# Renumbered MLP units, a merged w_in transfer and a new order in a fused attention and MLP kernel

## The chip, the core and the metric

The kernel runs on one core of a Trainium2 chip. The metric is the device time of one execution in microseconds (us); lower is better.

## The reference

Attention with normalized q and k over 8 batches of 12 heads (448 positions, head width 64), and then an MLP with a hard-swish gate on the 3584 x 768 result. All inputs and the output are float32.

```python
q_n, k_n = rmsnorm(q, g_q), rmsnorm(k, g_k)          # over the last axis
scores = (1.0 / np.sqrt(64)) * np.matmul(q_n, k_n.transpose(0, 1, 3, 2))
attn = softmax(scores)
x = np.matmul(attn, v).transpose(0, 2, 1, 3).reshape(3584, 768)
h = x @ w_in                                          # w_in: 768 x 2048
g = h * np.clip(h + 3.0, 0.0, 6.0) / 6.0
out = g @ w_out                                       # w_out: 2048 x 768
```

## The kernel before

The work goes by pairs of heads: 6 pairs a batch, 48 in all. For a pair, SyncE loads q, k and v (tiles `qk` and `vf`), squares are taken (tile `sq`, line 364 on ACT, 366 on POOL), DVE sums them (`ssq`, lines 488 and 454), ACT makes the inverse roots with a logarithm and an exponential (`rs`, lines 430 and 433), and q and k are scaled to bf16 (`qks`, line 369, on POOL or DVE). They are transposed to `T`, for the early pairs by TensorE (line 542) and copies out of PSUM (lines 352 and 360), for later pairs by a DMA transpose from SyncE's queue (line 561). The scores (lines 617 and 594) go to the PSUM tiles `S` and `X`, ACT takes their exponential (`eT`, lines 622 and 600), and the product with the values (`va`, with a column of ones for the sum) goes to `XF` or `X` (lines 639 and 680). DVE divides (line 655 or 699), and the result, transposed, is `xT`, the MLP's input (lines 664 and 715 on TensorE, 706 by DMA).

The first batch is done in two halves of 224 query positions, so that the MLP can begin early. Its hidden units are made by `h_first` (line 753): eight calls c = 0 to 7 for each half, each for two blocks of 128 units, so 224 columns to a matmul. All other batches use `h_group` (line 772): one block of 128 units, 448 columns. ACT and DVE then make the gate (lines 731 and 734) and write `gT`, with the hidden units on the partitions. `y_group` (line 794) multiplies 128 rows of `gT` with `w_out`, 16 blocks of 128 units, in two halves of 384 output columns, and the sum is copied to `y` and stored (lines 350, 352 and 815).

Both weight matrices are loaded once by GpSimd's queue, which turns float32 into bf16 on the way: w_in in four transfers of 512 columns (line 825), w_out in four transfers of 512 rows (line 830). In w_out, hidden unit c * 512 + f * 128 + p lies on partition p, so a partition receives four separate rows of 768 from one transfer. The blocks of units of w_in are 128 neighbouring columns:

```python
f0 = (2 * c + f) * 128
em(nc.tensor.matmul(out=ps()[:, f * SH:(f + 1) * SH], lhsT=w_in_sb[:, kt, f0:f0 + 128], ...))
```

No instruction is emitted where its function stands. Every step is entered in a `Plan` with what it reads and writes and the engines that it may run on. At the end `plan.emit(ORDER)` emits the 2386 steps in the order of a list written out in the file, each on the engine that the table `WAY` gives (0, the first of its list, where it isn't named). `em` ties each instruction to the one before it on the same engine, so that each engine, and each DMA queue, runs its steps strictly in that order. A step that waits holds up all that is queued behind it on its engine.

Where TensorE has nothing to do at the start, 30 matmuls on zeros are entered (`warm`, line 382), and 32 more (`idle`, line 375) in the first batch's value products.

Of the kernel before, what the change touches and what calls it, by code (L numbers as in the profile page):

```python
# [9 lines left out]
BF16 = mybir.dt.bfloat16  # L10
# [13 lines left out]
    53: 1, 54: 1, 61: 1, 63: 2, 68: 1, 69: 1, 83: 1, 84: 1, 90: 2, 95: 1, 101: 1, 121: 1, 122: 1, 128: 2,  # L24
    148: 1, 155: 2, 212: 1, 230: 1, 248: 1, 358: 1, 386: 1, 387: 1, 393: 2, 462: 1, 469: 1, 481: 1, 486: 1,
    523: 1, 531: 2, 553: 1, 560: 2, 573: 1, 589: 2, 608: 1, 618: 1, 624: 2, 653: 2, 664: 1, 738: 1, 770: 1,
    776: 2, 795: 1, 821: 1, 822: 1, 860: 2, 886: 2, 921: 1, 949: 1, 982: 1, 1005: 1, 1010: 1, 1024: 1, 1049:
    1, 1056: 1, 1067: 1, 1082: 2, 1108: 1, 1140: 2, 1151: 1, 1166: 1, 1177: 1, 1269: 1, 1285: 1, 1286: 1,
    1292: 1, 1317: 1, 1324: 2, 1350: 2, 1361: 1, 1369: 1, 1370: 1, 1376: 1, 1408: 2, 1419: 1, 1434: 1, 1445:
    1, 1469: 1, 1497: 1, 1530: 1, 1553: 1, 1565: 1, 1572: 2, 1589: 1, 1597: 1, 1604: 2, 1624: 1, 1630: 2,  # L30
    1641: 1, 1649: 1, 1656: 2, 1673: 1, 1682: 1, 1688: 1, 1714: 1, 1725: 1, 1754: 1, 1785: 1, 1817: 1, 1822:
    1, 1872: 1, 1892: 1, 1898: 2, 1917: 1, 1918: 1, 1924: 2, 1949: 1, 1956: 1, 1964: 1, 1979: 2, 1987: 1,
    2011: 1, 2039: 1, 2067: 1, 2072: 1, 2095: 1, 2100: 1, 2107: 1, 2108: 1, 2114: 2, 2143: 1, 2159: 1, 2160:
    1, 2166: 1, 2195: 1, 2250: 1, 2281: 1, 2345: 1, 2350: 1, 2362: 1, 2374: 1,
# [3 lines left out]
    9, 20, 8, 21, 22, 11, 23, 10, 24, 25, 14, 26, 13, 27, 53, 17, 31, 55, 32, 16, 33, 28, 54, 91, 34, 56,  # L38
    58, 57, 35, 68, 92, 61, 36, 59, 12, 70, 60, 29, 69, 62, 212, 15, 73, 71, 214, 64, 72, 119, 74, 37, 83,
    30, 66, 213, 76, 38, 39, 118, 65, 84, 40, 75, 67, 41, 230, 85, 18, 102, 77, 104, 103, 93, 42, 94, 79,  # L40
    215, 81, 43, 146, 80, 86, 44, 95, 45, 82, 87, 145, 105, 96, 129, 88, 46, 19, 122, 231, 131, 121, 89,
    224, 47, 63, 48, 97, 49, 232, 120, 98, 106, 130, 110, 111, 99, 107, 108, 112, 233, 132, 113, 109, 114,
    100, 123, 156, 216, 50, 148, 51, 149, 133, 115, 157, 135, 52, 78, 134, 116, 158, 136, 124, 0, 90, 217,
    137, 234, 125, 172, 159, 117, 138, 150, 139, 126, 140, 173, 164, 174, 141, 165, 142, 127, 151, 160, 235,
    166, 152, 175, 161, 153, 162, 143, 167, 163, 144, 101, 188, 168, 190, 169, 154, 248, 176, 128, 180, 189,
    218, 178, 170, 181, 177, 182, 219, 191, 183, 179, 171, 200, 184, 236, 220, 185, 201, 202, 221, 250, 245,
    155, 192, 186, 193, 203, 340, 222, 225, 187, 303, 251, 204, 223, 226, 194, 304, 249, 195, 237, 305, 242,
    196, 205, 359, 252, 197, 306, 238, 206, 243, 239, 315, 198, 240, 316, 227, 339, 207, 199, 317, 208, 228,
    241, 307, 253, 209, 308, 318, 327, 254, 341, 246, 309, 310, 271, 255, 328, 272, 367, 210, 273, 360, 311,
    329, 211, 229, 342, 312, 347, 343, 330, 319, 147, 256, 320, 344, 313, 321, 322, 314, 348, 274, 257, 349,  # L50
    361, 345, 331, 332, 350, 258, 370, 333, 334, 323, 1, 371, 324, 372, 275, 335, 259, 325, 276, 336, 362,
    373, 374, 489, 326, 337, 263, 375, 338, 363, 397, 387, 364, 351, 376, 398, 378, 352, 377, 353, 354, 379,
    365, 355, 399, 386, 356, 401, 264, 400, 357, 402, 380, 2, 388, 500, 358, 381, 403, 501, 405, 346, 265,
    406, 404, 407, 408, 389, 490, 382, 277, 502, 409, 383, 506, 390, 503, 410, 384, 266, 391, 385, 411, 267,
    507, 268, 412, 278, 504, 508, 3, 505, 512, 283, 513, 392, 509, 491, 510, 535, 284, 511, 525, 514, 269,
    515, 516, 524, 517, 492, 270, 518, 493, 285, 519, 537, 520, 366, 286, 279, 538, 494, 521, 280, 536, 526,
    291, 495, 281, 522, 541, 292, 523, 282, 533, 543, 293, 539, 260, 287, 527, 540, 294, 368, 288, 544, 528,
    261, 542, 545, 529, 289, 546, 393, 547, 247, 548, 290, 564, 582, 497, 566, 549, 565, 299, 550, 244, 530,
    300, 567, 395, 551, 295, 532, 301, 552, 572, 553, 498, 302, 570, 554, 296, 573, 394, 571, 421, 297, 583,
    568, 593, 595, 569, 298, 422, 423, 4, 555, 424, 594, 413, 414, 415, 496, 425, 596, 416, 531, 417, 5,  # L60
    418, 574, 419, 426, 575, 556, 601, 427, 420, 599, 618, 576, 428, 429, 602, 584, 430, 557, 577, 559, 431,
    433, 578, 585, 600, 432, 434, 558, 579, 607, 586, 437, 435, 580, 617, 438, 581, 436, 597, 439, 6, 605,
    441, 598, 606, 588, 440, 442, 608, 628, 443, 603, 7, 630, 604, 445, 444, 587, 619, 446, 631, 609, 610,
    646, 447, 611, 636, 629, 612, 637, 449, 647, 613, 620, 614, 659, 450, 660, 737, 448, 615, 634, 738, 453,
    616, 635, 451, 750, 632, 452, 657, 633, 454, 739, 458, 658, 648, 638, 621, 459, 740, 623, 460, 649, 741,
    622, 650, 748, 639, 749, 640, 641, 743, 663, 455, 751, 642, 643, 461, 651, 456, 262, 462, 652, 590, 644,
    457, 470, 645, 562, 465, 742, 561, 664, 466, 369, 754, 591, 756, 560, 661, 471, 760, 662, 467, 770, 665,
    626, 666, 757, 667, 769, 668, 625, 472, 669, 795, 396, 670, 473, 655, 589, 796, 671, 474, 468, 654, 672,
    755, 771, 786, 752, 782, 753, 482, 761, 483, 772, 783, 777, 797, 758, 499, 780, 773, 759, 484, 775, 745,
    469, 485, 821, 774, 798, 762, 781, 486, 763, 764, 765, 854, 812, 822, 477, 766, 624, 799, 677, 800, 767,  # L70
    478, 534, 823, 853, 746, 808, 806, 784, 809, 778, 479, 787, 801, 592, 807, 855, 678, 844, 480, 785,
    1017, 832, 481, 824, 834, 825, 788, 679, 829, 789, 879, 673, 680, 835, 768, 790, 653, 791, 1018, 833,
    674, 813, 685, 563, 675, 792, 802, 793, 686, 627, 826, 676, 810, 803, 687, 840, 838, 856, 464, 811, 681,
    827, 688, 804, 1019, 682, 857, 859, 656, 814, 683, 815, 816, 845, 794, 839, 693, 880, 684, 817, 841,
    694, 818, 744, 747, 819, 689, 1020, 695, 858, 870, 866, 696, 836, 867, 690, 881, 1075, 701, 888, 691,
    702, 837, 896, 692, 864, 776, 892, 703, 842, 882, 697, 843, 704, 830, 698, 488, 883, 709, 885, 699, 887,
    846, 1021, 865, 700, 710, 820, 1023, 871, 847, 711, 848, 705, 1050, 893, 712, 861, 849, 706, 1049, 850,
    1076, 851, 717, 707, 852, 890, 884, 708, 1030, 868, 1051, 718, 869, 713, 1040, 719, 897, 872, 891, 873,
    874, 720, 875, 487, 714, 1052, 1031, 876, 877, 725, 715, 878, 1028, 894, 716, 726, 895, 1077, 721, 1029,
    722, 860, 1078, 898, 723, 899, 1036, 727, 1034, 724, 900, 1053, 1035, 901, 1054, 729, 902, 903, 1037,  # L80
    730, 1022, 728, 904, 1032, 731, 1060, 1062, 1055, 1061, 733, 732, 1041, 734, 1025, 1033, 1134, 905, 886,
    1083, 735, 1038, 1066, 828, 1079, 1086, 1063, 736, 906, 1080, 909, 1039, 463, 1081, 1088, 907, 910,
    1109, 908, 1042, 862, 1101, 911, 1043, 1044, 1026, 1087, 913, 912, 1133, 831, 1045, 1089, 914, 1046,
    475, 917, 1135, 1067, 1092, 918, 915, 1047, 919, 1102, 1057, 916, 1112, 1114, 1027, 1064, 1103, 920,
    1065, 805, 922, 1110, 921, 1160, 923, 1058, 1068, 1093, 1048, 1069, 1113, 924, 925, 779, 929, 926, 889,
    1070, 1104, 1105, 1124, 1118, 1115, 1106, 1071, 930, 1072, 1285, 1073, 933, 1107, 931, 1084, 934, 1119,
    932, 863, 1159, 1090, 1120, 935, 476, 1144, 937, 1136, 1091, 936, 1150, 938, 1161, 941, 939, 1074, 1094,
    1056, 940, 1095, 942, 1162, 1286, 945, 943, 1142, 1121, 1096, 944, 1097, 946, 1098, 1024, 1099, 950,
    1137, 1163, 1145, 1125, 1165, 947, 1287, 1146, 1138, 1170, 1116, 1147, 948, 1139, 1117, 951, 949, 952,
    1317, 1318, 1176, 1288, 1122, 1172, 1123, 1082, 957, 1319, 1100, 953, 1151, 958, 1289, 954, 1290, 1126,  # L90
    1320, 1141, 959, 1127, 961, 1294, 1171, 1164, 960, 1128, 1129, 1173, 962, 1130, 1344, 1308, 1131, 965,
# [870 lines left out]
```

## Time and profile before

| | |
|---|---|
| median of 3 runs | 423.66 us (423.53 to 423.99) |
| the profiled execution | 423.13 us, its span 421.4 us |
| instructions in the span | 9981 |
| TensorE matmul, busy | 413.0 us (98%) |
| ACT, busy | 288.3 us (68%) |
| DVE, busy | 233.1 us (55%) |
| POOL, busy | 168.8 us (40%) |
| granted TensorE clock | 0.999 |
| DMA, mean rate | 161 GB/s |

PE is TensorE's matmul side and PEld its weight loads, which run beside the matmuls. DVE is VectorE, ACT ScalarE, POOL GpSimd, SP SyncE. A q behind the name (POOLq, SPq) is an engine's queue that issues DMAs. "L753" is line 753 of the kernel. q0 is the DMA queue that GpSimd fills (the weights), q1 the one of SyncE and ACT. Busy times of a group are the time in which at least one of its instructions runs; matmuls overlap, so that a busy time divided by a count is the distance from one to the next, and the mean duration beside it is longer. Line numbers of the kernel after are larger by 1 to 9 from line 262 on.

### The profile page before, as it was taken

The page shows a single profiled execution, that of the slowest core. Times are in us where ns is not written, and L with a number is a line of the kernel's source. Part 1 is how long each engine was busy: PE and PEld are TensorE (multiplying, and loading weights), DVE is VectorE, ACT ScalarE, POOL GpSimd, SP SyncE. Part 2 cuts the span into 40 slices and gives each one's busy share as a digit, 9 for nine tenths or more (in the row PEclk, how much of TensorE's full clock was granted, in tenths as well). Part 3 has the DMA queues.
Part 4 walks back from the last instruction along what each step waited for, and adds up shares of the span by engine and source line. Part 5 has one row for each costly group of instructions (what it writes and reads, how often), then busy time and mean ns, then how long its engine had stood idle before and what let it go on. Part 6 is the DMA issues. An engine that isn't in the chain of part 4 may idle for free.

```text
span 421.4 us, 9981 instructions
## 1 busy us (share of the span) xinstructions
PE 413.0 (98%) x3959; PEld 243.8 (58%) x3960; DVE 233.1 (55%) x474; ACT 288.3 (68%) x527; POOL 168.8 (40%) x189
## 2 busy tenths in 40 slices
PE   7899999999999999999999999999999999999996
PEld 3566886555545555555555555555655556555565
DVE  5987776588875667536554754447345333333210
ACT  6999887678887988788767876677765662133201
POOL 3999596478374554427344143043210100000000
PEclk9999999999999999999999999999999999999999
DMA  7999999999779799568495683747350601120034
GB/s 241 319 282 196 258 216 177 275 268 271 178 194 252 193 252 242 111 154 211 115 224 160 164 206 73 135 154 166 82 93 12 143 2 47 30 81 27 8 107 114
DMA packets 98979, 67.77 MB, mean 161 GB/s; under 512 B 53204, under 2 KB 95476, under 8 KB 98932
## 3 DMA queue, kind: packets, MB, share of 16 engines
q1 hardware_dynamic: 93296, 60.50, 56.9%
q0 software_dynamic: 5248, 6.29, 9.0%
q8 instruction: 31, 0.51, 0.5%
q10 hardware_dynamic: 388, 0.34, 0.3%
q14 instruction: 16, 0.13, 0.1%
HBM read 50.23 MB, written 11.01 MB: 145 GB/s over the span
## 4 chain that ended last, share of the span: by engine, by line
PE 82%; DMA 7%; ACT 5%; DVE 2%; issue 1%; POOL 1%; SPq 1%; POOLq 0%; ACTq 0%; DVEq 0%
PE M L772 27%; PE M L794 25%; PE X L680 9%; PE S L594 5%; PE M L753 4%; DMA qk<-in_k_dram 4%; PE S L794 4%; PE X L594 3%; DMA T<-qks 2%; PE X L772 1%; ACT sq L364 1%; DMA out_dram<-y 1%; ACT eT L600 1%; ACT eT L622 1%; PE S L617 1%
## 5 line engine op out<-in xcount | busy, mean ns | idle before, releaser
L794 PE MATMUL M<-w_out_sb,gT 128*128 128x384 bf16 x752 | 139.3, 326 | 0.2 <-DMA w_out_sb<-in_moe_w_out_dram 0.2
L772 PE MATMUL M<-xT,w_in_sb 128*128 128x448 bf16 x618 | 135.0, 353 | 0.1
L369 POOL TENSOR_TENSOR qks<-qk,rs 112x512 bf16<-112x512 f32 (+1 forms) x91 | 91.0, 1019 | 107.3 <-ACT rs L433 77.2
L794 PEld LDWEIGHTS <-gT 128*128 128x128 bf16 x912 | 84.5, 98 | 59.5 <-issue 7.6
L734 DVE SCALAR_TENSOR_TENSOR gT<-ts,M 128x448 bf16<-128x448 f32 x119 | 73.2, 616 | 72.1 <-ACT ts L731 71.6
L600 ACT ACTIVATE eT<-S 112x896 bf16<-112x896 f32 x112 | 100.3, 915 | 15.7 <-PE S L594 8.5
L731 ACT ACTIVATE ts<-M 128x448 f32<-128x448 f32 x119 | 64.7, 545 | 42.7 <-PE M L772 29.2
L772 PEld LDWEIGHTS <-w_in_sb 128*128 128x128 bf16 x672 | 60.2, 98 | 56.3 <-issue 10.5
L366 POOL TENSOR_TENSOR sq<-qk 112x512 f32<-112x512 f32 (+1 forms) x57 | 58.0, 1024 | 52.9 <-DMA qk<-in_q_dram 29.7
L680 PEld LDWEIGHTS <-eT 112*128 112x128 bf16 x1344 | 52.7, 97 | 14.5 <-issue 2.0
L600 ACT ACTIVATE eT<-X 112x896 bf16<-112x896 f32 x56 | 51.3, 917 | 13.3 <-PE X L594 12.2
L680 PE MATMUL X<-va,eT 112*128 112x65 bf16 x1344 | 56.0, 194 | 0.1
L454 DVE TENSOR_REDUCE ssq<-sq 112x16 f32<-112x1024 f32 x42 | 50.9, 1213 | 6.1 <-POOL sq L366 4.7
L594 PE MATMUL S<-T 64*128 64x448 bf16 x224 | 34.0, 353 | 0.1
L352 DVE COPY y<-M 128x384 f32<-128x384 f32 x26 | 14.5, 556 | 30.9 <-PE M L794 30.8
L699 DVE TENSOR_TENSOR xn<-X,rd 112x512 bf16<-112x512 f32 x42 | 28.9, 689 | 1.3 <-DVE rd L696 0.2
L696 DVE RECIPROCAL rd<-X 112x8 f32<-112x8 f32 x42 | 8.6, 206 | 34.5 <-PE X L680 28.6
L594 PEld LDWEIGHTS <-T 64*128 64x128 bf16 x336 | 12.9, 94 | 24.5 <-issue 17.2
L364 ACT ACTIVATE sq<-qk 112x512 f32<-112x512 f32 (+1 forms) x40 | 23.0, 586 | 2.8 <-DMA qk<-in_k_dram 2.5
L350 ACT COPY y<-M 128x384 f32<-128x384 f32 x21 | 10.0, 477 | 19.4 <-PE M L794 19.2
L753 PE MATMUL M<-xT,w_in_sb 128*128 128x224 bf16 x192 | 22.9, 259 | 0.0
L794 PE MATMUL S<-w_out_sb,gT 128*128 128x384 bf16 (+1 forms) x128 | 22.6, 316 | 0.0
(87 smaller groups left out, 300.9 us busy)
## 6 DMA issues: line engine op xcount, KB each, us to landing
qk<-in_k_dram SPq DMA_DIRECT2D x45, 256.0 KB, 4.8
qk<-in_q_dram SPq DMA_DIRECT2D x45, 256.0 KB, 4.7
vf<-in_v_dram SPq DMA_DIRECT2D x43, 256.0 KB, 4.8
w_in_sb<-in_moe_w_in_dram POOLq DMA_DIRECT2D x4, 768.0 KB, 8.4
w_out_sb<-in_moe_w_out_dram POOLq DMA_DIRECT2D x4, 768.0 KB, 9.5
out_dram<-y SPq DMA_DIRECT2D x7, 336.0 KB, 3.5
out_dram<-y SPq DMA_DIRECT2D x8, 288.0 KB, 3.3
out_dram<-y SPq DMA_DIRECT2D x8, 240.0 KB, 2.8
```

What stands on the lines that cost most here:

```text
L366: em(nc.gpsimd.tensor_tensor(out=out, in0=in_, in1=in_, op=A_MULT))
L369: em((nc.vector if e == DVE else nc.gpsimd).tensor_tensor(out=out, in0=in_, in1=by.unsqueeze(3).to_broadcast(list(in_.shape)), op=A_MULT))
L454: em(nc.vector.tensor_reduce(out=ssq[:].rearrange("p i n -> p (i n)"), in_=sq[:].rearrange("p i (n d) -> p (i n) d", d=D), axis=AX_X, op=A ...
L594: em(nc.tensor.matmul(out=ps[:, a, 0:S], lhsT=qkT[r, S + t * TP:S + t * TP + 128], rhs=qkT[r, 0:S], start=True, stop=True))
L600: em(nc.scalar.activation(out=eT[:, t, 0:S2].rearrange("p (a s) -> p a s", a=2), in_=ps[0:TP, :, 0:S], func=EXP, bias=0.0, scale=1.0))
L680: em(nc.tensor.matmul(out=X_ps[:, a, i * E1:(i + 1) * E1], lhsT=eT[:, t, c:c + 128], rhs=va[:, a, t, :], start=(t == 0 and i == 0), stop=( ...
L699: em(nc.vector.tensor_tensor(out=xn[:].rearrange("p i a d -> p a i d"), in0=view()[:, :, :, 0:D], in1=rd[:].unsqueeze(3).to_broadcast([TP, ...
L731: em(nc.scalar.activation(out=ts[:], in_=ps()[:, 0:S], func=RELU, bias=0.5, scale=1.0 / 6.0))
L734: em(nc.vector.scalar_tensor_tensor(out=out, in0=shape(ts[:]), scalar=1.0, in1=shape(ps()[:, 0:S]), op0=A_MIN, op1=A_MULT))
L753: em(nc.tensor.matmul(out=ps()[:, f * SH:(f + 1) * SH], lhsT=w_in_sb[:, kt, f0:f0 + 128], rhs=xT[:, kt, z * SH:(z + 1) * SH], start=(kt == ...
L772: em(nc.tensor.matmul(out=ps()[:, 0:S], lhsT=w_in_sb[:, kt, f * 128:(f + 1) * 128], rhs=xT[:, kt, :], start=(kt == 0), stop=(kt == NKT - 1)))
L794: em(nc.tensor.matmul(out=ps()[:, 0:nc0], lhsT=gT[:, f, i * 128:(i + 1) * 128], rhs=w_out_sb[:, f, c0:c0 + nc0], start=(f == 0), stop=(f = ...
```

## The change

It has three parts.

1. The hidden units are numbered anew. In w_out, unit c * 512 + 4 p + f now lies on partition p, so that a partition's four rows of one transfer lie one after another in memory: 12 KB in one piece. To match, the block f of 128 units takes every fourth column of w_in, from column f mod 4 of chunk f div 4 on (new function `hid`). The weights of the 864 hidden matmuls are thus read with a step of four elements.
2. `w_in` is three tiles instead of one, and is loaded in three transfers instead of four: 512, 1024 and 512 columns (`WIN`).
3. `ORDER` and `WAY` are written anew. There is one step fewer, so all numbers from 2 on move by one. Apart from that, the last 383 steps stand as before, and so do the first 23; in between the order differs, most in the first half. 72 steps run on another engine: of note are the casts of v (GpSimd has 16 of them instead of 7), and a few squares, copies and scalings.

The lists of numbers in `ORDER` and `WAY` are left out here.

```diff
-    w_in_sb = const.tile([128, NKT, DFF], BF16, name="w_in_sb")
+    WIN = ((0,), (1, 2), (3,))
+    w_in_sb = [const.tile([128, NKT, len(cs) * 512], BF16, name=f"w_in_sb{cs[0]}") for cs in WIN]
...
+    def hid(f, kt):
+        c, r = divmod(f, 4)
+        i = next(i for i, cs in enumerate(WIN) if c in cs)
+        c -= WIN[i][0]
+        return w_in_sb[i][:, kt, c * 512 + r:(c + 1) * 512:4]
...
-                        f0 = (2 * c + f) * 128
                         em(nc.tensor.matmul(
-                            out=ps()[:, f * SH:(f + 1) * SH], lhsT=w_in_sb[:, kt, f0:f0 + 128],
+                            out=ps()[:, f * SH:(f + 1) * SH], lhsT=hid(2 * c + f, kt),
...
-                        out=ps()[:, 0:S], lhsT=w_in_sb[:, kt, f * 128:(f + 1) * 128],
+                        out=ps()[:, 0:S], lhsT=hid(f, kt),
...
-        for c in range(4):
-            def f_i(_, c=c):
-                cols = slice(c * 512, (c + 1) * 512)
+        for i, cs in enumerate(WIN):
+            def f_i(_, i=i, cs=cs):
+                cols = slice(cs[0] * 512, (cs[-1] + 1) * 512)
                 em(nc.gpsimd.dma_start(
-                    out=w_in_sb[:, :, cols], in_=moe_w_in[:, cols].rearrange("(k p) n -> p k n", p=128)))
-            plan.add("w_in", [POOL], f_i, [], [("w_in", c)])
+                    out=w_in_sb[i][:], in_=moe_w_in[:, cols].rearrange("(k p) n -> p k n", p=128)))
+            plan.add("w_in", [POOL], f_i, [], [("w_in", c) for c in cs])
...
-                    in_=moe_w_out[c * 512:(c + 1) * 512, :].rearrange("(f p) n -> p f n", p=128)))
+                    in_=moe_w_out[c * 512:(c + 1) * 512, :].rearrange("(p f) n -> p f n", f=4)))
```

280 rows, old and new, of tables (ORDER, WAY) are left out of this document.

## The prediction

> **What bounds the kernel now.** First the page's engine line, then stages of the span, then the waits of the matmul engine, then the chain of waits.
>
> ```profile
> PE 413.0 (98%) x3959; PEld 243.8 (58%) x3960; DVE 233.1 (55%) x474; ACT 288.3 (68%) x527; POOL 168.8 (40%) x189
> ```
>
> TensorE is busy 413.0 of 421.4 us, so 8.4 us at most are visibly idle. The stages tell where. The columns are stage, length, then busy time (and instructions) of PE, weight load, DVE, ACT and POOL, granted clock, DMA share and GB/s.
>
> ```profile
> 0.00:20.00 20.00, 16.07 (x161) 8.49 (x162) 14.29 (x46) 16.09 (x43) 13.30 (x28) 1.00 0.92 284
> 20.00:40.00 20.00, 19.45 (x331) 13.70 (x328) 16.76 (x52) 19.84 (x34) 19.78 (x25) 1.00 1.08 245
> 40.00:60.00 20.00, 19.87 (x280) 17.51 (x278) 15.92 (x31) 17.45 (x35) 14.57 (x16) 1.00 1.02 234
> 80.00:100.00 20.00, 19.84 (x202) 10.77 (x200) 17.32 (x36) 16.72 (x32) 15.09 (x16) 1.00 1.18 262
> 100.00:150.00 50.00, 50.00 (x480) 26.97 (x478) 35.65 (x67) 43.02 (x79) 29.01 (x30) 1.00 0.88 218
> 400.00:421.40 21.40, 18.20 (x128) 11.82 (x126) 2.03 (x4) 2.23 (x5) 0.00 (x0) 0.97 0.38 109
> ```
>
> The idle time is 3.93 us in the first 20 us and 3.20 us at the end (the last output copies and stores, which the change leaves alone). From 100 us on PE is full. So the only places where an order can win or lose are the first 40 us, and small gaps up to 100 us. In the second stage PE still reads 19.45 of 20, but ACT (19.84) and POOL (19.78) are full too: there the exponentials and the normalized q and k are made just as fast as those two engines can, and PE's matmuls stand ready behind them. The waits of PE name the same producers:
>
> ```profile
> PE M L542 <- POOL qks L369: 1.6, 2, 1.4
> PE S L617 <- ACT eT L622: 0.4, 1, 0.4
> PE M L794 <- DMA w_out_sb<-in_moe_w_out_dram: 0.2, 1, 0.2
> ```
>
> And the chain of waits in order of time runs on ACT from 6.56 to 18.19 us without a break of note, then on PE, then once more on three ACT exponentials:
>
> ```profile
> 6.56 0.63 ACT sq L364
> ...
> 16.58 1.61 ACT eT L622 x2
> 18.19 0.10 ACT rs L430
> 18.34 0.39 PE M L542 x4
> ...
> 38.45 2.54 ACT eT L600 x3
> ```
>
> So ACT sets the pace from 6.6 to about 41 us, POOL is next to it, and after that PE's own work, which the change doesn't alter in kind or number (the matmuls and weight loads of both programs are the same in count), is the bound.
>
> **Part 1: strided weights.** With the renumbering each of the 864 weight loads of w_in (192 at L753, 672 at L772) takes every fourth column, a step of 8 bytes, where it took 128 neighbours. No row of before has a strided load; the nearest ones:
>
> ```profile
> L680 PE MATMUL X<-va,eT 112*128 112x65 bf16 x1344 | 56.0, 194 | 0.1
> L772 PE MATMUL M<-xT,w_in_sb 128*128 128x448 bf16 x618 | 135.0, 353 | 0.1
> L753 PE MATMUL M<-xT,w_in_sb 128*128 128x224 bf16 x192 | 22.9, 259 | 0.0
> L753 PEld LDWEIGHTS <-w_in_sb 128*128 128x128 bf16 x192 | 16.8, 98 | 2.2 <-issue 2.2
> ```
>
> At L680 one load and one matmul together pass in 56.0/1344 = 41.7 ns, so a contiguous load costs at most that in a stream. A matmul of L753 occupies 22.9/192 = 119 ns, one of L772 135.0/618 = 218 ns, and the next load goes beside it. A strided load could thus be 2.9 times slower at L753 and 5.2 times at L772 for nothing. Bounds: 0, if it is up to 2.9 times slower; if it were four times slower (every fourth element used, one fetch each), 167 - 119 = 48 ns on 192 loads = +9.2 us, and still nothing at L772. It can't gain, as the load is hidden already. I take 0, the end within which even a load slowed 2.9 times lies. [...]
>
> **Part 2: the transfers of the weights.** The two questions are how long they hold the DMA engines, and who waits. Transfers in two stretches, 35 to 44 us (w_in) and 57 to 70 us (w_out):
>
> ```profile
> q0 software_dynamic: 1692, 1.70, 117.4%
> ...
> q0 software_dynamic: 1810, 2.71, 115.1%
> ```
>
> A w_in packet reads 2 KB and takes 1.174 x 9 x 16 / 1692 = 100 ns, a w_out packet reads 3 KB and takes 1.151 x 13 x 16 / 1810 = 132 ns: 32 ns a KB and 36 ns on top. Four rows in a packet: 36 + 12 x 32 = 420 ns against 4 x 132 = 528, so all of w_out needs 512 x 420 / 16 / 1.15 = 11.7 us instead of 14.7. The middle half of w_in: 768 packets of 164 ns, 6.7 us instead of 8.2. That is an estimate of 4.5 us of DMA time less, and 0 if packets this long are cut up again. But hardly anything waits for it: PE's wait for w_out is 0.2 us in all, and that is what I count, -0.2.
>
> [...]
>
> **Part 3: ACT and POOL in the first 40 us.** The new order and engine table change who does what there. Their rows before:
>
> ```profile
> 19.24 0.61 ACT L350 CAST gT<-vf 112x512 bf16<-112x512 f32 x1
> 19.75 0.41 ACT L364 ACTIVATE sq<-qk 112x256 f32<-112x256 f32 x1
> ...
> 34.94 0.34 ACT L350 COPY xT<-XF 128x224 bf16<-128x224 bf16 x1
> 35.35 0.92 ACT L600 ACTIVATE eT<-S 112x896 bf16<-112x896 f32 x1
> ```
>
> Up to the first full exponential (35.35 us) ACT loses that cast and that copy to DVE and gains one 256-wide square: -0.61 - 0.34 + 0.41 = -0.54 us. DVE takes them with 16.76 of 20 us busy. From there to the sixteenth two more squares leave ACT (another 1.0 us), when ACT is at 17.45 of 20 and no longer the pace. Bounds -0.9 to 0; I take -0.5, the row's own sum.
>
> At the very start POOL takes the first k scaling from DVE and a half square from ACT, in time when it waits; ACT puts the 256-wide square of the second pair ahead of the first pair's second root, which holds the first q half back by about 0.3 us; and DVE's late reduction leaves the place right ahead of the first k copy:
>
> ```profile
> 7.43 0.71 ACT L364 ACTIVATE sq<-qk 112x256 f32<-112x256 f32 x2
> ...
> 8.26 0.41 DVE L488 TENSOR_REDUCE late_ssq<-sq 112x4 f32<-112x256 f32 x1
> 8.59 0.44 DVE L360 TENSOR_SCALAR gT<-M,gp_t 128x448 bf16<-128x448 bf16 x1
> ```
>
> 0.3 us later on one operand of the first scores, 0.33 us (8.26 to 8.59) sooner on the other, which came last: I count 0, bounds -0.3 to +0.3.
>
> On POOL there is one w_in issue fewer, of 0.88 us (row below), in the stage in which POOL is full. PE's longest wait is for POOL, but POOL is seldom on the chain after it; I take half, -0.4, between -0.88 and 0. Nine more casts of values go to POOL, nearly all after 50 us, where the rows leave it 21 of 50 us; they cost nothing as long as that room lasts.
>
> **Sum.** 0 - 0.2 - 0.5 + 0 - 0.4 = -1.1 us. The profiled execution took 423.13 us (span 421.4 and 1.7 around it), 0.5 under the median of 423.66, inside what runs differ by; 423.13 - 1.1 = 422.0 profiled, and 422.6 as a median. About 0.2% (0.85 us) is what can be told from no change.
>
> **Rivals.**
> *Slower: the merged transfer lands too late.* Units 4 to 11 now all wait for one landing. Before:
>
> ```profile
> 28.60 2.04 POOL L369 TENSOR_TENSOR qks<-gT,rs 112x512 bf16<-112x512 f32 x2
> 30.59 0.88 POOL L825 DMA_DIRECT2D w_in_sb<-in_moe_w_in_dram  x1
> ...
> DMA to landing us min/median/max: 7.5/8.4/9.1
> ...
> 38.80 0.74 PE L753 MATMUL M<-xT,w_in_sb 128*128 128x224 bf16 x6
> 39.47 0.36 PE L594 MATMUL X<-T 64*128 64x448 bf16 x2
> ...
> 52.12 2.04 POOL L366 TENSOR_TENSOR sq<-qk 112x512 f32<-112x512 f32 x2 [2.02 <-DMA qk<-in_k_dram]
> ```
>
> The second transfer is issued at 30.59 and first used at 38.80, hardly 0.7 us after the fastest landing. In the new order the double one stands ahead of those two scalings, so at about 28.6 us; it needs 7.5 us plus a second 768 packets (4.1 us at 1692 in 9 us), less up to 1.5 us for fewer packets: landing at 38.7 to 40.2. Its first use is moved behind two more score pairs, to about 39.5 to 40. So it is just in time, and every us that POOL comes later is a us of PE idle. With the quick landing (10.1 us after the issue) PE waits from an issue at 29.4 us on, and the sign turns from about 31.4 on, when 2 us of idle outweigh the gain. With a slip like POOL's wait for an input load at 52.12, 2.0 us, on top of the late landing (40.2 + 2.0 against 39.6), PE stands 2.6 us, and the total is 423.66 - 1.1 + 2.6 = 425.2. For it: margins are under 1 us. Against: PE waited for no w_in before, and the order moved its use back. Chance 0.19.
>
> *No change.* PE reads 19.45 of 20 where ACT and POOL are full, so what they gain may just turn into longer waits for PE's bank; then only w_out's 0.2 us remain, 423.4. Chance 0.25.
>
> *Strided loads cost.* +9.2 - 1.1 gives 431.8; 0.06, since only a load slowed more than 2.9 times begins to show.
>
> *More.* If all of POOL's and ACT's relief counts (0.88 + 0.9 + 0.3 + 0.2 = 2.3), 421.4. Part of the forecast's case.
>
> **How the numbers follow.** Forecast case (faster, 421.0 to 422.8, likeliest 422.6) 0.47; no change 0.25; late transfer 0.19; strided loads 0.06; another producer late by over 0.9 us somewhere in 40 to 100 us, 0.03. Faster 0.47, same 0.25, slower 0.28. The range goes from 421.0 (a little under the full relief) to 425.2 (the late transfer); out of it are the strided loads, the worse half of the late cases, and a tail below.
>
> **What would show it.** Right: the LDWEIGHTS at the w_in lines stay near 98 ns and the 224-wide matmuls near 119 ns each; ACT's first full exponential starts about 0.5 us before 35.35; PE's wait for w_out is gone; q0 has some 3,000 packets less and its 12 KB packets take near 420 ns. Wrong: a wait of PE for w_in near 39 to 41 us; L753's busy time well over 22.9 us; PE idle in 20 to 40 us over 0.55; or a new wait for qks or T in 60 to 100 us.

## The result and the profile after

| | before | after |
|---|---|---|
| median | 423.53 us (422.98 to 423.99) | 426.23 us (425.28 to 426.81) |
| ratio | | 1.0061 [1.0048, 1.0074] |
| the profiled execution | 423.13 us, span 421.4 | 426.81 us, span 425.0 |

The changed kernel is 2.7 us slower. A second set of its runs gave 426.54 us, ratio 1.0077 [1.0048, 1.0106]. The forecast was 422.6, the range 421.0 to 425.2. The engine line of the page of after:

```profile
PE 413.7 (97%) x3960; PEld 253.4 (60%) x3960; DVE 230.6 (54%) x469; ACT 287.7 (68%) x524; POOL 170.5 (40%) x194
```

TensorE's matmul side is 413.7 us busy where it was 413.0, in a span that is 3.6 us longer: the work is nearly the same, and PE stands idle longer. The stages of after (columns as in the prediction) say where:

```profile
20.00:40.00 20.00, 19.13 (x322) 12.99 (x320) 17.32 (x56) 19.74 (x34) 18.21 (x23) 1.00 0.99 217
40.00:60.00 20.00, 18.62 (x265) 16.66 (x266) 13.37 (x24) 16.42 (x31) 15.36 (x18) 1.00 1.05 272
60.00:80.00 20.00, 18.93 (x217) 13.48 (x216) 12.06 (x24) 14.19 (x30) 12.33 (x15) 1.00 0.98 202
100.00:150.00 50.00, 48.41 (x476) 27.91 (x475) 33.30 (x62) 42.67 (x78) 32.68 (x34) 1.00 0.93 225
```

Before, 60 to 80 us read:

```profile
60.00:80.00 20.00, 19.83 (x231) 13.27 (x232) 11.12 (x21) 14.42 (x26) 12.80 (x15) 1.00 0.98 204
```

Against before, PE was busy 1.25 us less from 40 to 60 us, 0.90 less from 60 to 80 and 1.59 less from 100 to 150. From 20 to 40 us it was 0.32 less, in the first 20 us 0.71 more (16.78 us). Three waits of PE that before did not have, or had at 0.2 and 0.3 us, answer to the three largest losses (columns: total us, times, longest):

```profile
PE M L761 <- DMA w_in_sb<-in_moe_w_in_dram: 1.8, 1, 1.8
PE X L595 <- DVE xn L700: 1.6, 1, 1.6
...
PE M L802 <- DMA w_out_sb<-in_moe_w_out_dram: 1.1, 1, 1.1
```

Together 4.5 us, against 0.5. The first is the merged transfer, whole on the chain of waits from GpSimd's issue to the matmul:

```profile
28.55 12.79 DMA w_in_sb<-in_moe_w_in_dram
41.34 0.05 issue
41.38 0.77 PE M L761 x6
```

The second is the last transfer of w_out. GpSimd issued it 4.3 us later than before, where the timeline reads:

```profile
61.83 0.80 POOL L830 DMA_DIRECT2D w_out_sb<-in_moe_w_out_dram  x1
```

GpSimd's timeline of after:

```profile
28.55 0.89 POOL L833 DMA_DIRECT2D w_in_sb<-in_moe_w_in_dram  x1
...
34.22 0.88 POOL L833 DMA_DIRECT2D w_in_sb<-in_moe_w_in_dram  x1
...
61.96 0.59 POOL L838 DMA_DIRECT2D w_out_sb<-in_moe_w_out_dram  x1
...
66.13 0.59 POOL L838 DMA_DIRECT2D w_out_sb<-in_moe_w_out_dram  x1
```

The weights' queue shows the late issue. In the two us from 66 on before moved 0.42 MB (columns: packets, MB, share of the 16 engines):

```profile
q0 software_dynamic: 287, 0.42, 116.1%
```

After, the same stretch and the one from 68 on:

```profile
q0 software_dynamic: 65, 0.36, 94.3%
...
q0 software_dynamic: 57, 0.29, 81.0%
```

The third wait is for one `xn`. Its writer on DVE was held by a transposing DMA, issued at 107.73 us behind four groups of loads and two stores on SyncE's queue. Experiment 8 is about it.

### The profile page after: what moved, and what is told of

Read it like the earlier page. It is cut to its first block, busy times and chain, and to the rows that moved or that the text cites. A ratio compares the mean times of both kernels' runs of the same rounds, so it can differ in the third digit from the quotient of the medians.

```text
span 425.0 us, 9984 instructions
## 1 busy us (share of the span) xinstructions
PE 413.7 (97%) x3960; PEld 253.4 (60%) x3960; DVE 230.6 (54%) x469; ACT 287.7 (68%) x524; POOL 170.5 (40%) x194
## 3 DMA queue, kind: packets, MB, share of 16 engines
q0 software_dynamic: 2928, 6.29, 8.2%
## 4 chain that ended last, share of the span: by engine, by line
PE 81%; DMA 10%; ACT 3%; POOL 3%; issue 1%; SPq 1%; DVE 0%; ACTq 0%; POOLq 0%; DVEq 0%
PE M L802 28%; PE M L780 27%; PE X L681 8%; PE S L595 5%; PE S L802 4%; DMA w_in_sb<-in_moe_w_in_dram 3%; ACT eT L623 2%; PE X L595 2%; DMA w_out_sb<-in_moe_w_out_dram 2%; DMA xT<-xn 2%; DMA gT<-in_k_dram 1%; POOL sq L367 1%; PE X L780 1%; DMA qk<-in_k_dram 1%; POOL qks L370 1%
## 5 line engine op out<-in xcount | busy, mean ns | idle before, releaser
L780 PEld LDWEIGHTS <-w_in_sb 128*128 128x128 bf16 x672 | 70.1, 114 | 48.9 <-issue 10.9
L732 ACT ACTIVATE ts<-M 128x448 f32<-128x448 f32 x119 | 64.7, 545 | 48.1 <-PE M L780 29.7
L367 POOL TENSOR_TENSOR sq<-qk 112x512 f32<-112x512 f32 (+1 forms) x55 | 56.1, 1027 | 64.8 <-DMA qk<-in_q_dram 25.3
L595 PE MATMUL S<-T 64*128 64x448 bf16 x224 | 34.3, 354 | 0.3 <-DVE T L353 0.3
L365 ACT ACTIVATE sq<-qk 112x512 f32<-112x512 f32 (+1 forms) x42 | 24.5, 589 | 3.9 <-DMA qk<-in_k_dram 3.5
L761 PE MATMUL M<-xT,w_in_sb 128*128 128x224 bf16 x192 | 23.1, 260 | 1.8 <-DMA w_in_sb<-in_moe_w_in_dram 1.8
```

The costliest lines, as they stand in the source:

```text
L365: em(nc.scalar.square(out=out, in_=in_))
L367: em(nc.gpsimd.tensor_tensor(out=out, in0=in_, in1=in_, op=A_MULT))
L595: em(nc.tensor.matmul(out=ps[:, a, 0:S], lhsT=qkT[r, S + t * TP:S + t * TP + 128], rhs=qkT[r, 0:S], start=True, stop=True))
L732: em(nc.scalar.activation(out=ts[:], in_=ps()[:, 0:S], func=RELU, bias=0.5, scale=1.0 / 6.0))
L780: em(nc.tensor.matmul(out=ps()[:, 0:S], lhsT=hid(f, kt), rhs=xT[:, kt, :], start=(kt == 0), stop=(kt == NKT - 1)))
```

## The experiments

The theory was: the merged transfer lands late, the last of w_out is issued late, and these two are the loss. Rivals: the strided numbering, the other moves of the order, the transposing DMA. Every ratio below is to the kernel before, run on the same chip. The four runs of 512 columns of w_in are called quarters 0 to 3; the merged transfer is quarters 1 and 2. In `ORDER` of the changed kernel step 1 is the merged transfer, step 2 the last quarter of w_in, and steps 3 to 6 are the transfers of w_out. The mean granted clock of an execution serves as a sign below: 3.4 us at half clock, as experiment 8 shows them, cost 1.7 us, which is 0.004 of the span and gives a mean of 0.996. An execution at 0.998 or above is called one at full clock; the kernel before stood at 0.999 or 1.0 in every execution whose clock is on record.

**1. The numbering alone.** On the kernel before, its order and four transfers kept:

```diff
-  lhsT=w_in_sb[:, kt, f * 128:(f + 1) * 128]
+  lhsT=hid(f, kt)     # w_in_sb[:, kt, c * 512 + r:(c + 1) * 512:4], one tile
...
-  moe_w_out[...].rearrange("(f p) n -> p f n", p=128)
+  moe_w_out[...].rearrange("(p f) n -> p f n", f=4)
```

> The kernel before with the new numbering alone: strided weight loads of w_in and 12 KB rows of w_out, but four transfers of w_in and the order of before. Theory (the loss is three new waits of TensorE, 1.8 + 1.1 + 1.6 us, all made by the order and the merged transfer): 423.5 us, within 0.5 of before; loads of 114 ns stay hidden, the w_out transfers land no sooner since both kernels moved some 205 KB of bf16 a us. Rival (strided loads slow the matmuls): 425 us or more, with the distance between 448-wide matmuls above 189 ns.

449.62 us, ratio 1.0608 [1.0582, 1.0634]. It did not measure the numbering. GpSimd's timeline shows why:

```profile
46.19 0.88 POOL L829 DMA_DIRECT2D w_in_sb<-in_moe_w_in_dram  x1 [10.86 <-PE XF L664]
57.28 0.88 POOL L829 DMA_DIRECT2D w_in_sb<-in_moe_w_in_dram  x1 [7.60 <-PE M L757]
```

The issues of quarters 2 and 3 waited 10.86 and 7.60 us for instructions of PE, and PE then 20.6 us for weights; its clock fell to a mean of 0.965. The reading that fits is that, with all of w_in in one tile, a strided slice counts as overlapping the neighbouring quarters. The changed kernel has a tile for each transfer. So once more, with four tiles:

```diff
+    w_in_sb = [const.tile([128, NKT, 512], BF16, name=f"w_in_sb{c}") for c in range(4)]
...
+        return w_in_sb[c][:, kt, r:512:4]
```

> The kernel before, its order and its four transfers of w_in untouched, each quarter in a tile of its own, and the new numbering with packets of four rows of w_out. With one tile for all quarters (the run of the numbering on the kernel before) GpSimd's issue of the third quarter stood until 46.19 us for a PE instruction and of the fourth until 57.28 us, where the kernel before issued them at 34.49 and 37.97: the program took the quarters for overlapping, and that run measured this. Theory (numbering costs nothing by itself): 423.5 us, 422.9 to 424.3, no wait of PE for w_in over 0.3 us, the 448-wide matmuls at 353 or 354 ns. Rival (strided weights cost PE time): 425 us or more, with a mean over 354 ns.

424.82 us, ratio 1.0014 [0.9996, 1.0032]: not told from 1, though the median lies above the 424.3 that the theory allowed. The waits of 10.86 and 7.60 us are gone with the single tile. No wait of PE for w_in or w_out is left, and the groups of its w_in lines read:

```profile
L776 PE MATMUL M<-xT,w_in_sb 128*128 128x448 bf16 x618 | 135.4, 354 | 0.0
L776 PEld LDWEIGHTS <-w_in_sb 128*128 128x128 bf16 x672 | 70.2, 114 | 48.4 <-issue 10.3
...
L757 PE MATMUL M<-xT,w_in_sb 128*128 128x224 bf16 x192 | 23.1, 260 | 0.0
L757 PEld LDWEIGHTS <-w_in_sb 128*128 128x128 bf16 x192 | 17.4, 114 | 2.2 <-issue 2.2
```

A strided weight load takes 114 ns where a plain one took 98, and the matmuls keep their distance by busy time over count (135.4/618 = 219 ns where it was 218, 23.1/192 = 120 where it was 119).

**2. The old numbering on the changed kernel**, order and merge kept:

```diff
-        return w_in_sb[i][:, kt, c * 512 + r:(c + 1) * 512:4]
+        return w_in_sb[i][:, kt, c * 512 + r * 128:c * 512 + (r + 1) * 128]
...
-  moe_w_out[...].rearrange("(p f) n -> p f n", f=4)
+  moe_w_out[...].rearrange("(f p) n -> p f n", p=128)
```

> The kernel after with the old numbering: contiguous loads, 3 KB rows of w_out; the merged w_in transfer and the new order stay. Theory (three waits): 426.2 us, within 0.5 of after, with all three waits still there, that for w_in near 1.8 us and that for w_out near 1.1. Rival (strided loads): back to 423.5.

428.24 us, ratio 1.0096 [1.0074, 1.0119]. The loss stays without the numbering, and is 1.7 to 2.0 us larger than that of the changed kernel, where the theory allowed 0.5:

```profile
PE M L802 <- DMA w_out_sb<-in_moe_w_out_dram: 2.5, 2, 2.3
PE M L761 <- DMA w_in_sb<-in_moe_w_in_dram: 2.0, 1, 2.0
```

Five of its six executions had a mean clock of 0.994 to 0.996; the one at full clock took 426.86 us. The profiled one lost 4 x 0.41 + 3 x 0.02 = 1.7 us by its clock from 43 us on, so half clock lasted 3.4 us. So half clock is much of the difference, and a longer wait for w_out (2.5 us against 1.1) may be the rest. That the larger packets help where a transfer is late is not excluded by this. Whether they are worth anything where nothing is late was asked on the mended kernel of experiment 5, with its middle half split and its last transfer of w_out earlier:

> The run with the split middle half and the earlier w_out, with the old numbering: plain 128-column weights and 3 KB packets (1.5 KB rows of w_out). It tells what the numbering brings where no transfer is late. Theory (the queue's byte rate does not depend on the packet size): 423.8 us within 0.8, waits for w_out within 0.5 us of those with the new numbering. Rival (packets of four rows do land sooner, and the old numbering had a wait of 2.5 us in the run of the old numbering): a wait of 1.5 us or more for w_out, 425 us or more.

423.74 us, ratio 1.0006 [0.9994, 1.0019], against 423.80 with the new numbering. Where nothing is late, the numbering neither costs nor brings time that these runs can tell. (A row of w_out in memory is 3 KB, not the 1.5 of that expectation.)

**3. The merge undone**, the order kept; both halves are issued one after the other at 28.3 us:

```diff
...
+                for c in cs:
+                    cols = slice(c * 512, (c + 1) * 512)
+                    em(nc.gpsimd.dma_start(out=w_in_sb[c][:], in_=moe_w_in[:, cols]...))
```

> The kernel after, with the middle half of w_in as two transfers of 512 columns issued one behind the other at the same place. Theory: the first half lands some 4 us before 41.3, TensorE's 1.8 us for w_in go, GpSimd has 0.9 us more to issue: 424.4 to 425.3. Rival (the wait only uses slack that is lost later anyway): 426.2.

425.11 us, ratio 1.0036 [1.0017, 1.0055]. The wait for w_in is gone, the longest wait is now another:

```profile
PE M L800 <- DMA w_out_sb<-in_moe_w_out_dram: 2.2, 1, 2.2
```

PE comes to the last of w_out 1.2 us sooner and waits there 1.1 us longer: more than half of the 1.8 us is given back to the second late transfer, which was issued 1.0 us sooner and landed only 0.1 us sooner (74.66 us, was 74.79).

**4. The merge alone**, on the kernel before (quarters 1 and 2 at the place of quarter 1, old order and numbering):

```diff
+    WIN = ((0,), (1, 2), (), (3,))
...
```

> The kernel before, its order and numbering, quarters 1 and 2 as one transfer where quarter 1 was issued, at about 30.6 us. Theory (the merged transfer lands 10 to 13 us after its issue, and PE uses quarter 1 at about 40): landing at 41 to 43.4, a wait of PE for w_in of 1 to 3.8 us, 424.5 to 427.5 us. Rival (the merge is harmless, the moved orders cost): 423.5 us within 0.8, no such wait over 0.5 us.

429.71 us, ratio 1.0134 [1.0112, 1.0155]. The wait was within what the theory gave, the total 2 us above its bound:

```profile
PE M L759 <- DMA w_in_sb<-in_moe_w_in_dram: 3.5, 1, 3.5
```

The rest of its loss is in the granted clock, told under experiment 8.

**5. Both mended**: the middle half split, and the last transfer of w_out (step 6) right behind the third:

```diff
-    5, 597, 439, ... 611, 630, 633, 448, 612, 6, 613,
+    5, 6, 597, 439, ... 611, 630, 633, 448, 612, 613,
```

> The changed kernel with the middle half in two transfers again, and the last transfer of w_out issued right behind the third, at about 62.6 us instead of 66.1. Theory (the two late transfers are most of the loss): the waits for w_in and of 2.2 us for the last of w_out go, 422.9 us, 422.3 to 424.2. Rival (the wait for w_out is set by the queue's rate, not by the issue): a wait for w_out of 2 us or more stays, 425 us. Second rival (the earlier transfer keeps the loads back and they become late): a new wait for inputs, 425 us or more.

423.80 us, ratio 1.0001 [0.9983, 1.0019], all twelve executions at full clock. With the two transfers earlier the loss is gone; PE's wait for the last of w_out is 0.6 us. The new order's other moves, its casts on GpSimd and the numbering together neither cost nor bring more than the 0.8 us that this interval leaves. (The earlier w_out with the merge kept is in experiment 7.) The issues of quarters 1 and 2 and the times to their landings:

```profile
28.15 1.72 POOL L832 DMA_DIRECT2D w_in_sb<-in_moe_w_in_dram  x2
...
DMA to landing us min/median/max: 9.0/10.5/11.9
```

So quarter 1 is there at 28.15 + 9.0 = 37.2 us, and quarter 2, issued half of 1.72 us later, at 29.0 + 11.9 = 40.9. That is 12.75 us after the first issue. Merged, both landed together, 12.8 us after their issue in the profile of after: the merge takes nothing off the later half and makes the first wait for it.

**6. The merged transfer issued earlier**, step 1 before step 253, at 26.6 us:

> The kernel after, with the merged transfer issued three GpSimd steps earlier (at about 26.0 instead of 28.55 us), nothing else moved. Theory: it lands at 38.8 to 39.5, so that the wait of 1.8 us shrinks to under 0.5, at the price of input loads that share the engines with it from 28 us on: 424.4 to 425.3. Rival (slack that is lost later anyway): 426.2; or worse, if the loads that it delays become the wait.

430.65 us, ratio 1.0140 [1.0109, 1.0171], a miss. The wait for w_in is gone, and PE stands for ACT, which waits for inputs that now come behind the weights: a load of k issued at 27.48 us landed 11.6 us later, and ACT did nothing from 38 to 39 us. The clock stood at half for 6.8 us besides, from 38.6 us on (3.4 us lost in the stages from 38 to 46 us).

```profile
PE S L543 <- ACT eT L623: 4.4, 2, 2.4
```

**7. The last quarter of w_in issued later.** Open was whether it, 5.7 us behind the merged transfer, takes that one's bandwidth:

```diff
-    399, 401, 378, 262, 2, 357, ... 507, 225, 512, 391,
+    399, 401, 378, 262, 357, ... 507, 225, 512, 2, 391,
```

> The changed kernel with the transfer of the last quarter of w_in issued three of GpSimd's operations later, at about 37.9 us instead of 34.2 (the kernel before issued it at 37.97). In the profile of the changed kernel the weights' queue moved 0.32, 0.40 and 0.43 MB in the two-us stretches from 32 us, in packets of 4 KB; from 38 us on the packets of the last quarter ran beside them (240 and 347 packets in a stretch after 208), and the merged transfer landed at 41.34, 12.8 us after its issue. Theory (the last quarter takes the merged one's bandwidth before it has landed): landing at about 39.5 to 40.2, PE's wait for w_in falls from 1.8 to 2.5 us to 0.7 or less, 425.0 us, 424.3 to 425.6. Rival (the merged transfer needs 12.8 us by itself, or the loads of the inputs take the freed bandwidth): landing and wait unchanged, 426.3 us within 0.6. Second rival (the last quarter is late instead): a wait for w_in near 50 us, 426 us or more.

425.56 us, ratio 1.0048 [1.0030, 1.0067]. The time is inside the theory's range, but its mechanism is there in small part at most. The chain of waits:

```profile
28.77 12.52 DMA w_in_sb<-in_moe_w_in_dram
```

The landing came 12.5 us after the issue, where the theory needed 10.7 to 11.4 (39.5 to 40.2 us); unmoved it was 12.8 us, and 13.5 in the second profile of the changed kernel (experiment 8). So the last quarter is not what makes the merged transfer long. The wait is 1.3 us instead of 1.8 because PE arrives later (its 1.3 us end at 41.34). With the earlier w_out added:

> The kernel of the run third_later with the last transfer of w_out right behind the third as well. Theory (both late transfers mended, with the merge and the numbering kept, and GpSimd's one issue less): 423.6 us, 422.8 to 424.4. Rival (the merge stays late): 425 us or more.

426.23 us, ratio 1.0064 [1.0041, 1.0087], though the profiled execution took 424.06 us with a wait for w_in of 0.8. The runs spread from 423.67 to 428.95. Two more executions with a profile:

> The kernel of the run third_later_wout once more, one execution with its profile: its twelve runs spread from 423.67 to 428.95 us, and the profiled one (424.06) was the second fastest. Theory (the merged transfer lands at a time that differs by some us between executions, and a long stand of PE leads to some us at half clock): an execution over 426 us shows a wait for w_in of 1.5 us or more, or a stretch of the granted clock at 0.5 after it; one under 424.5 us shows neither. Rival (the spread comes from elsewhere): an execution over 426 us with a wait for w_in under 1 us and the clock at 1.0.

> As the look before, a further execution of the same kernel, with the same two readings.

424.48 us with a wait for w_in of 1.5, and 425.78 with 1.4, in both at a clock of 1.0. The landing came 11.8, 12.5 and 12.4 us after its issue in the three. The length of the wait does not explain the spread. The mean clock explains a part: of the twelve executions, three were at full clock (423.67, 424.06 and 426.06 us), and nine at 0.995 or 0.996 (425.15 to 428.95), which is 1.7 us or a little more lost in each. No execution over 426 us was profiled, so what lowers the clock in them, and what spreads the nine by 3.8 us, stays open. What can be said is that these two moves of its neighbours do not mend the kernel with the merge kept.

**8. The third wait.** The transposing DMA of that `xn` (step 819) ahead of the loads from step 803 on:

> The changed kernel with only the transposing transfer of one xn (at 107.73 us in its profile, its xn written by 101.86) issued before the four loads and one store that stood ahead of it on SyncE's queue. Theory (that place costs PE its wait of 1.6 us at 115.6): this wait goes, 424.6 us, 424.0 to 425.3. Rival (PE works ahead and meets the next wait instead): 426.2 us within 0.6.

428.05 us (425.27 to 430.29), ratio 1.0085 [1.0051, 1.0119], a miss. The wait for `xn` is gone and the median is not shorter. Four of the six executions had a mean clock of 0.991 to 0.996, which hides what the move itself does; the two at full clock took 425.27 and 425.83 us. The profiled execution shows a price of the first wait that the profile of after had not shown (stages, the granted clock is the third number from the end):

```profile
40.00:43.00 3.00, 1.26 (x15) 1.27 (x16) 1.10 (x2) 1.59 (x4) 2.04 (x3) 1.00 1.19 220
43.00:46.00 3.00, 3.00 (x40) 2.44 (x39) 1.61 (x5) 1.82 (x4) 1.78 (x2) 0.51 0.86 202
46.00:47.00 1.00, 1.00 (x10) 0.89 (x9) 0.60 (x2) 0.55 (x1) 0.78 (x2) 0.75 0.61 168
```

After a stand of 2.0 us for w_in TensorE ran at half clock: 3 x 0.49 + 0.25 = 1.7 us lost once more, so the half clock lasted 3.4 us. The run of the merge alone had a mean of 0.83 over 40 to 60 us behind its 3.5 us, which is 20 x 0.17 = 3.4 us lost in 6.8 us at half clock, a part of it within the stand; with the 3.5 us that covers the 5.7 us of its median. Does the changed kernel pay this too?

> The changed kernel unchanged, once more. PE's wait for the merged transfer was 1.78 us in its first profile, and the granted clock stayed at 1.0; in the run of the earlier transposing transfer the same wait was 1.95 us, and the clock stood at 0.50 from about 43 to 46.5 us, which by itself is 1.6 us. Theory (a stand of about 2 us leads now and then to some us at half clock, which is part of the price of the late transfer): the runs spread over 425 to 429 us, with a median between 425.5 and 428. Rival (the halved clock belongs to other kernels only): all runs within 425.3 to 426.8 us.

426.54 us (424.84 to 429.59). The profiled one of them, 427.04 us, had a longer stand and kept its clock:

```profile
43.00:46.00 3.00, 3.00 (x56) 2.75 (x54) 2.04 (x5) 2.01 (x4) 1.23 (x2) 1.00 0.76 188
...
PE M L761 <- DMA w_in_sb<-in_moe_w_in_dram: 2.5, 1, 2.5
```

So the length of the stand alone does not decide: 2.5 us went without it, 2.0 us did not. The spread speaks for the theory, and so do the mean clocks: of the changed kernel's twelve executions in both sets, three were at 0.995 or 0.996 (426.38, 427.70 and 429.59 us). Of this kernel no such execution was profiled. The other nine, at full clock, have a median of 426.23 us: the loss is there without the clock, and half clock comes on top now and then. What makes the clock drop after one stand and not after another was not shown.

The second profile of the changed kernel has also no wait for `xn` at all, and its span (425.2) is that of the first (425.0): PE was already later by its longer first wait. The wait of 1.6 us is thus not a third part of the loss of its own, as far as one profile shows it; the mended kernel, at the time of before, has it at 0.2 us with the DMA in its old place.

**9. Towards a better version.** In the mended kernel PE still stood 0.9 us at 29.7 us, for a scaling that GpSimd runs behind the two issues. Quarter 2 was moved to quarter 3 at 34.3 us:

```diff
-    WIN = ((0,), (1, 2), (3,))
+    WIN = ((0,), (1,), (2, 3))     # each quarter still a transfer of its own
...
```

> As the run with the split middle half and the earlier w_out, but quarter 2 of w_in is issued with quarter 3 at about 34.6 us (the kernel before: 34.49) and no longer behind quarter 1 at about 29. Theory (each transfer in time, and the POOL time of the second issue out of the way of the keys' scaling, for which PE stood 0.86 us at 29.7): 423.0 us, 422.3 to 423.9, so the same as before or 0.2% faster. Rival (quarter 2 now lands too late): a wait for w_in near 44 us, 425 us or more.

426.13 us, ratio 1.0062 [1.0046, 1.0078], a miss: the wait at 29.7 is gone, and two others stand for it.

```profile
PE M L759 <- DMA w_in_sb<-in_moe_w_in_dram: 0.7, 2, 0.4
PE X L681 <- POOL va L355: 0.7, 1, 0.7
```

> The kernel of the run regrouped, with the second transfer of w_out issued right behind the first as well, at about 54 us. Theory: the wait of 0.6 us for the last of w_out at 73 us goes, 422.6 us, 421.9 to 423.6. Rival (the weights then take the queue from the inputs): a new wait for inputs between 60 and 80 us, 424 us or more.

426.62 us, ratio 1.0071 [1.0050, 1.0091]; the wait for `va` grows to 1.6 us. The new waits are smaller than the loss, all but one of these twelve executions were at full clock, and what else these two lose was not found. No version ran faster than the kernel before.

## Why the prediction was wrong

**The failed step is the landing of the merged transfer**, told as the rival "lands too late" with a chance of 0.19. Its issue (forecast 28.6, was 28.55) and PE's arrival (39.5 to 40, was 39.6) were right; the landing was put at 38.7 to 40.2 and came at 41.34, in the second profile 2.5 us after PE. Its three terms, by the runs:

- 7.5 us for the first half was the time from an issue at 30.59, landing at 38.1. Issued 2.4 us sooner, in the mended kernel, the same quarter took 9.0 us and was there only 0.9 us sooner. This is the term that was mis-sized: from 30 to 32 us the loads still had most of the DMA engines, as the profile of after shows:

```profile
q1 hardware_dynamic: 553, 0.53, 79.6%
q0 software_dynamic: 24, 0.05, 18.6%
```

- 4.1 us for the second half was good: 40.9 - 37.2 = 3.7.
- Up to 1.5 us less for fewer packets was not there: 12.8 us after the issue merged, 12.75 as two. In the two us from 36 on the queue of after moved 0.43 MB:

```profile
q0 software_dynamic: 208, 0.43, 112.5%
```

Before, with packets of half the size, it was 0.40:

```profile
q0 software_dynamic: 402, 0.40, 120.8%
```

With the measured terms, 9.0 + 3.7 = 12.7 us, and 28.55 + 12.7 = 41.3.

**The price of the rival** was tied to a slip of 2.0 us that did not happen, and was not needed: without any slip PE stood 1.8 to 2.5 us. That half clock may follow a stand, as in experiment 8 (1.7 us lost after one of 2.0 us), was not counted.

The forecast was 1.1 us faster and the result is 2.7 slower, 3.8 us apart. By the first profile that is the wait for w_in (1.8), w_out (0.9 instead of -0.2, so 1.1), and the 0.9 us of part 3 that did not come. The 0.71 us won in the first 20 us and the wait for `xn` are left out, so this is an account and no proof.

**Part 2, w_out: -0.2 became +0.9.** The sum took the time per packet for the bound and did not follow where the last issue went. It came 4.3 us later, the queue ran thin, and PE's wait grew from 0.2 to 1.1. The estimate of 11.7 instead of 14.7 us fell with it: full, the queue moved 0.42 MB in two us with either packet. A 12 KB packet took 474 ns in the median, where 420 were worked out.

**Part 1 was right, at 0.** No row of before showed a strided load, and the sign of loads near 98 ns did not come: a load took 114. It cost nothing, as the matmuls kept their distance. The 218 and 119 ns taken for a matmul are a little long, since busy time over count takes in the end of each run: on the chain six in a row of the 448-wide ones take 1.14 us before and after, 190 ns each, and six of the 224-wide ones 0.58 us before and after, 97 ns each. For the former the prediction's argument holds, a load of 114 ns lies under its matmul. For the latter the load takes longer than that distance, and why it cost nothing even there was not shown.

**Part 3, -0.5 and -0.4, is not in the time.** The mended kernel has all of the relief of ACT and equals before: its PE is busy 16.85 us in the first 20 us, 0.78 more than before, and 18.72 in the next 20, 0.73 less. One issue fewer on GpSimd can be had only with the merge, and the merge costs more. The first full exponential began at 35.05 us in after, 0.3 sooner, not 0.5. The rival "no change" described what these parts do.

**The signs that it named.** Of those against it, a wait of PE for w_in near 39 to 41 us came, and PE's idle time from 20 to 40 us was 0.87 us, over its 0.55; a new wait for `qks` or `T` in 60 to 100 us did not come. Of those for it, loads near 98 ns and no wait for w_out did not come. The weights' queue had 2320 packets less (2928, before 5248): the "some 3,000" is a slip, its own counts give 2304.

## What to carry to other kernels

A transfer that is just in time is not one to merge, because its first half then lands with its second (here 12.8 us after the issue, where alone it took 9.0). Work out the margin from the landings under the traffic at the new issue time, not from the quickest one at the old place. When an order is written anew, follow every DMA issue in it to its new time before costing its packets; here a transfer issued 4.3 us later outweighed anything that larger packets brought. Give separately loaded parts of a weight separate tiles, above all before strided slices are used (experiment 1: 449.62 us with one tile, 424.82 with four). Read the mean clock of every execution, not of the profiled one alone: here it showed which ones had lost time to the clock.

## What the runs showed of the hardware

- A weight load with a column step of 8 bytes took 114 ns, a plain one 98. The matmuls beside them kept their distance on the chain, before and after 97 ns at 224 columns and 190 at 448.
- From 34 to 40 us (w_in) and from 58 to 64 us (w_out) the weights' queue moved 0.38 to 0.43 MB (as written, in bf16) in two us, before with packets of 2 and 3 KB, after with packets of 4 (from 38 us on also 2) and 12 KB.
- Half clock came in stretches of 3.4 us (experiments 2 and 8, with a PE stand of 2.0 us), of 6.8 us (experiment 4, with one of 3.5, and 6), and of 10.2 us (the first kernel of experiment 1, from 35.5 us on, with a stand of 8.4 us); after a stand of 2.5 us it stayed away in the second profile of the changed kernel.
